# Scores of a head pair as products of 192 and 384 columns on two row halves, and an earlier copy of the attention product

## The chip, the cores and the metric

The kernel runs on one core of a Trainium2 chip. The metric is the device time of one execution in microseconds (us); the median of several executions counts.

## The reference

Top-k attention (8 batches, 8 heads, 576 rows, head size 64, k = 32), followed by a gated feed-forward part. Cut to what matters:

```python
scores = scale * np.matmul(q, k.transpose(0, 1, 3, 2))
kth = np.partition(scores, -32, axis=-1)[..., -32:-31]
scores = np.where(scores >= kth, scores, -1e9)
attn = exp(scores - max); attn /= attn.sum(-1)
x = (attn @ v), heads side by side                    # (8, 576, 512)
h = np.maximum(x @ w_in, 0)                           # 512 -> 1024
conv = conv_w[0]*h[s-1] + conv_w[1]*h[s] + conv_w[2]*h[s+1]
out = (h * sigmoid(conv)) @ w_out                     # 1024 -> 512
```

## The kernel before

Two heads form a pair, 32 pairs in all. A pair's 2 x 576 rows are cut into nine tiles of 128 rows: tiles 0, 2, 4, 6 hold 128 rows of the first head, tiles 1, 3, 5, 7 the same rows of the second, and tile 8 the last 64 rows of both heads, one head on each half of the partitions. That makes 288 tiles, and `iteration(it)` runs once for each: it writes out by hand, engine by engine, the work of several tiles that are at different stages. No scheduler moves anything, the written order is the engines' order. The feed-forward part of a finished batch is spread over the later iterations by a credit (`FEED`, `PE_CAP`); what is left over runs behind the last tile.

The names that matter here, in the order in which a tile meets them:

- `scores` (TensorE, L206, L211, L214): at an even tile it makes the scores of that tile and of the next, one head on rows 0 to 63 of the array, the other on rows 64 to 127, since a head has 64 elements. Both heads' first or last 512 columns are one product each (L211). The 64 columns that are left of each head are made together by one product over all 128 rows (L214), from an extra 128 columns of `k` that hold each head's edge beside zeros. An f32 product runs as two passes, each with its weight load. Tile 8 goes over quarters of the array (L206).
- `s_ps` is a PSUM tile of three banks of 512 columns. The first head's scores stand in columns 0 to 575, the second's in 960 to 1535, and in the middle bank between the two edges lie two corners of 128 columns, used in turn for the product of attention and values.
- `evacuate` (ScalarE, L220) copies a tile's 576 scores to `rows`; from there VectorE looks for the 32nd largest (L227, L247, L249, L275, L279), ScalarE makes `side` (L260) and the exponential (L272), GpSimd multiplies (L265), VectorE masks and sums (L285).
- `transposes` (TensorE, L298) puts the weighted tile into `pt`, `transposed` (ScalarE, L303, L305) copies it to `pT`, `tails` and `tailed` (L311, L315) do the same for the last columns.
- `av` (TensorE, L329, L332) multiplies `pT` with the values, two column halves at a time, into a corner of `s_ps`; `av_out` (ScalarE, L340) copies the corner to `xt` one iteration later.

In an iteration ScalarE runs `sides`, `evacuate`, `transposed`, `av_out`, then the exponential; TensorE runs `transposes`, feed-forward products (L396, L546), `tails`, `scores`, `av`. The scores of an even tile have to wait until ScalarE has read the middle bank, which means until the `xt` copy of the same iteration.

Of the kernel before, what the change touches and what calls it, by code (L numbers as in the profile page):

```python
# [21 lines left out]
P = 128  # L22
# [34 lines left out]
BANK = 512  # L57
# [8 lines left out]
def attend_and_feed(ctx: ExitStack, tc: tile.TileContext, q, k, v, weights, out, shared, finish=None):  # L66
    nc = tc.nc
    exact = finish is None
    v_main, v_tail = v
    B, NPAIR, _, S = q.shape  # L70
    D = P // 2
# [4 lines left out]
    SH = S // 2  # L76
    NI = S // P
    TAIL = S - NI * P
    MAIN = NI * P
    NBLK = 2 * NI + 1  # L80
    scale = 1.0 / float(D) ** 0.5
# [32 lines left out]
    s_ps = ps.tile([P, 3 * BANK], F32, name="s_ps", bufs=1)  # L114
# [3 lines left out]
    def bank(name):  # L118
        return ps.tile([P, BANK], F32, name=name, tag=name, bufs=1)

    def corner(i, w=P):
        return s_ps[:, BANK + TAIL + i * P:BANK + TAIL + i * P + w]

    scratch = []

# [72 lines left out]
    def scores(t):  # L198
        kx, qx = t.pc.nat["k"], t.pc.nat["q"]
        i = t.j // 2  # L200
        rows_of = [slice(h * D, (h + 1) * D) for h in range(2)]
        if t.j == 2 * NI:
            for to, n in ((0, MAIN), (MAIN, TAIL)):
                for h, d in enumerate(rows_of):
                    at = (to + TAIL * h) % S
                    nc.tensor.matmul(s_ps[rows_of[1 - h], to:to + n], lhsT=qx[d, 0:TAIL], rhs=kx[d, at:at + n],  # L206
                                     start=True, stop=True)
        elif t.j % 2 == 0:
            at = slice(TAIL + i * P, TAIL + (i + 1) * P)
            for h, d in enumerate(rows_of):  # L210
                nc.tensor.matmul(s_ps[:, 2 * h * BANK:(2 * h + 1) * BANK], lhsT=qx[d, at],  # L211
                                 rhs=kx[d, h * TAIL:h * TAIL + MAIN], start=True, stop=True)
            ends = s_ps[:, BANK:2 * BANK].rearrange("p (a c) -> p a c", c=TAIL)[:, 0:BANK // TAIL:BANK // TAIL - 1]
            nc.tensor.matmul(ends, lhsT=qx[:, at], rhs=kx[:, S:S + 2 * TAIL], start=True, stop=True)  # L214

    def evacuate(t):
        t.row = rows[:, t.n % XBUFS]
        x = t.x = t.row[:, 8:S + 8]
        at = 3 * BANK - S if t.j < 2 * NI and t.j % 2 else 0
        nc.scalar.copy(out=x, in_=s_ps[:, at:at + S])  # L220

    def chunk_ops(t):
# [77 lines left out]
    def transposed(t):  # L300
        st, j, tp = t.st, t.j, t.tp
        if j < 2 * NI:
            nc.scalar.copy(out=st.pT[:, j % 2], in_=tp.rearrange("p (i c) -> p i c", i=NI))  # L303
        else:
            nc.scalar.copy(out=st.pT[:, :, :, 0:TAIL].rearrange("p h i c -> p i h c"),  # L305
                           in_=tp.rearrange("p (i h c) -> p i h c", i=NI, h=2))
# [262 lines left out]
    parts, extra, outs_late, unready, ends = [], [], [], [], {}  # L569
# [57 lines left out]
    tiles = {}  # L627
# [83 lines left out]
    def iteration(it):  # L711
        nonlocal av_next, out_next, rec_next
        n = it + 3
        state.it = it
        pre, tA, tB, tC = (tiles.get(i) for i in (it + 2, it, it - 1, it - 2))
        tX, tD, tE = tiles.get(it - 3), tiles.get(it - 4), tiles.get(it - 5)
# [11 lines left out]
        if n < NT:  # L728
# [3 lines left out]
            t = Box()  # L732
# [5 lines left out]
            sides(tC)  # L738
        if pre is not None:
            evacuate(pre)  # L740
        if tE is not None:
            transposed(tE)
        outs, out_next = out_next, []
        for st in outs:
            av_out(st)
            if st.i == NI:
                norm_wait.append((it + NORM_LAG, st.pc))

        if exact:
            a_ops, b_ops = [], list(exact_ops(tB)) if tB is not None else []  # L750
# [67 lines left out]
        while pool_tasks and state.pool > 0.2 and pool_tasks[0][0] <= it:  # L818
# [3 lines left out]
            _, c, fn = pool_tasks.popleft()  # L822
# [11 lines left out]
        for it in range(-3, NT + 6):  # L834
            iteration(it)
    if finish is not None:
        finish(corner(2, 1)[0:1])
    while expands or contracts or any(x.waiting for x in lanes) or pool_tasks or tanh_next or tanh_now or gates:
        it += 1
        iteration(it)  # L840
# [67 lines left out]
def _layout(inputs):  # L908
    import numpy as np

    q, k, v = (np.asarray(inputs[name]) for name in "qkv")
    B, H, S, D = q.shape
    main = S // P * P

    def pairs(x, swapped):
        x = x.transpose(0, 1, 3, 2)
        heads = [np.concatenate([x[:, h, :, main:], x[:, h, :, :main]], axis=-1) if swapped(h) else x[:, h]
                 for h in range(H)]
        return np.stack(heads, axis=1).reshape(B, H // 2, 2 * D, S)

    ends = np.zeros((B, H // 2, 2, D, 2, S - main), k.dtype)
    for h in range(2):
        ends[:, :, h, :, h] = k[:, h::2, main:].transpose(0, 1, 3, 2)
    ends = ends.reshape(B, H // 2, 2 * D, -1)
    tails = np.zeros((B, H // 2, 2, S - main, 2, D), v.dtype)
    for h in range(2):
        tails[:, :, h, :, h] = v[:, h::2, main:]

    arrays = {
        "q": pairs(q, lambda h: True),  # L930
        "k": np.concatenate([pairs(k, lambda h: h % 2 == 1), ends], axis=-1),
        "v_main": v[:, :, :main].reshape(B, H // 2, 2, main // P, P, D).transpose(0, 1, 4, 2, 3, 5),
        "v_tail": tails.reshape(B, H // 2, 2 * (S - main), 2, D),
        "w_in": inputs["moe_w_in"],
        "conv_w": np.asarray(inputs["moe_conv_w"]).reshape(3, -1, P).transpose(2, 0, 1).reshape(P, -1),
        "w_out": inputs["moe_w_out"],
    }
    arrays = {name: np.ascontiguousarray(a) for name, a in arrays.items()}
    return {name: a.view(np.int64) if a.dtype == np.float64 else a for name, a in arrays.items()}
# [22 lines left out]
```

## Time and profile before

| | |
|---|---|
| three runs | 1128.35, 1132.26, 1133.33 us; median 1132.26 |
| profiled execution | 1132.29 us, of which 1130.4 us are the span in the trace |
| TensorE matmuls busy | 1022.8 us (90%) |
| VectorE busy | 1026.6 us (91%) |
| ScalarE busy | 994.4 us (88%) |
| GpSimd busy | 891.7 us (79%) |
| mean granted TensorE clock | 0.976 |

Busy time says how much of a stretch an engine was at work. A list of waits says who stood still and what ended it. The chain is the one path of work that ended last: time off the chain can vanish without moving the end. "issue" is time for which the profile shows no wait, and the ends of matmuls are modelled.

### The profile page before, as it was taken

To read this page: it belongs to the slowest core of one execution; us is meant where nothing else is said; L and a number is where in the kernel's file an instruction comes from. 1 tells how busy PE (TensorE), PEld (TensorE's weight loads), DVE (VectorE), ACT (ScalarE), POOL (GpSimd) and SP (SyncE) were. 2 spreads that over 40 slices of the span, in tenths; PEclk is the share of its full clock that TensorE was granted. 3 is DMA by queue.
4 is the path that set the end of the run, shared out by engine and by line. 5 is a ranking of instruction groups with operands and counts; after the bars stand their busy time and mean duration, and the time that the engine had idled before them with its cause. 6 is when DMAs were issued, how large, how long until landed. Compare 5 with 4: busy or idle time off the path is not lost.

```text
span 1130.4 us, 27192 instructions
## 1 busy us (share of the span) xinstructions
PE 1022.8 (90%) x7970; PEld 758.3 (67%) x7970; DVE 1026.6 (91%) x5768; ACT 994.4 (88%) x2342; POOL 891.7 (79%) x1078
## 2 busy tenths in 40 slices
PE   4656578889999999999999899999999999999997
PEld 1434345667677777777777677777677677777885
DVE  5998999999999999999999999999999999998651
ACT  5998888899999999999999999999999999998442
POOL 6999845879878897998887897978978897898300
PEclk9997888999999999999999999999999999999999
DMA  7321011111211101111111111111111110110001
GB/s 256 97 86 47 2 46 47 47 47 47 66 48 56 44 30 50 56 56 57 56 56 57 56 34 44 46 56 56 57 56 56 56 54 28 44 31 21 31 28 41
DMA packets 51694, 60.75 MB, mean 54 GB/s; under 512 B 9776, under 2 KB 30544, under 8 KB 51536
## 3 DMA queue, kind: packets, MB, share of 16 engines
q1 hardware_dynamic: 51536, 58.91, 16.4%
q8 instruction: 66, 1.08, 0.4%
q14 instruction: 92, 0.75, 0.2%
HBM read 49.31 MB, written 9.58 MB: 52 GB/s over the span
## 4 chain that ended last, share of the span: by engine, by line
PE 45%; DVE 36%; ACT 14%; POOL 2%; issue 2%; DMA 0%; SPq 0%; ACTq 0%; POOLq 0%
DVE cand L227 11%; PE mc L546 9%; DVE e L285 8%; PE me L396 8%; PE s_ps L329 6%; DVE z L275 6%; PE pt L298 5%; PE s_ps L211 5%; ACT weights_ps L272 3%; DVE cand L249 3%; PE s_ps L206 2%; PE s_ps L214 2%; ACT rows L220 2%; PE weights_ps L546 2%; DVE hot L279 2%; DVE rows L247 2%
## 5 line engine op out<-in xcount | busy, mean ns | idle before, releaser
L227 DVE MAX8 cand<-rows 128x8 f32<-128x82 f32 (+1 forms) x2016 | 453.0, 239 | 0.1
L265 POOL TENSOR_TENSOR z<-rows,side 128x579 f32<-128x579 f32 x288 | 347.5, 1207 | 127.5 <-ACT side L260 108.5
L285 DVE SCALAR_TENSOR_TENSOR e<-rows,kth,weights_ps 128x576 f32<-128x576 f32 x288 | 230.4, 800 | 0.2
L272 ACT ACTIVATE weights_ps<-rows,z 128x576 f32<-128x576 f32 x288 | 220.0, 764 | 8.2 <-DVE e L285 2.9
L260 ACT ACTIVATE side<-rows 128x576 bf16<-128x576 f32 x288 | 224.4, 779 | 0.3
L396 PE MATMUL me<-x_hi,wi 128*128 128x322 f32 (+1 forms) x928 | 218.6, 309 | 1.1 <-ACT g L410 1.1
L220 ACT COPY rows<-s_ps 128x576 f32<-128x576 f32 x288 | 183.5, 637 | 38.0 <-PE s_ps L332 21.0
L275 DVE MAX8 z<-z 128x8 f32<-128x576 f32 x288 | 214.2, 744 | 1.5 <-POOL z L265 1.5
L211 PE MATMUL s_ps<-k,q 64*128 64x512 f32 x512 | 151.4, 669 | 59.8 <-ACT xt L340 45.1
L298 PE MATMUL pt<-ident,e 128*128 128x128 f32 x1152 | 188.0, 287 | 2.1 <-DVE e L285 1.8
L546 PE MATMUL mc<-wo,split 128*128 128x512 f32 x684 | 187.1, 407 | 0.0
L329 PE MATMUL s_ps<-pT,vn 128*64 128x128 f32 (+1 forms) x2560 | 168.0, 276 | 12.7 <-ACT rows L220 12.6
L329 PEld LDWEIGHTS s_ps<-pT,vn 128*64 128x64 f32 x2560 | 131.9, 141 | 49.0 <-ACT rows L220 22.6
L396 PEld LDWEIGHTS me<-x_hi,wi 128*128 128x128 f32 x928 | 157.1, 189 | 2.3 <-ACT g L410 2.1
L303 ACT COPY pT<-pt 128x512 f32<-128x512 f32 x256 | 152.5, 596 | 4.2 <-PE pt L298 4.2
L298 PEld LDWEIGHTS pt<-ident,e 128*128 128x128 f32 x1152 | 131.9, 145 | 27.6 <-issue 14.7
L396 PE MATMUL me<-x_lo,wi 128*128 128x258 f32 (+1 forms) x464 | 138.4, 298 | 0.0
L546 PEld LDWEIGHTS mc<-wo,split 128*128 128x128 f32 x684 | 120.1, 189 | 20.0 <-issue 0.2
L429 POOL TENSOR_SCALAR t<-g,cr 128x256 f32<-128x256 f32 (+1 forms) x222 | 114.4, 515 | 0.0
L247 DVE MAX8 rows<-cand 128x8 f32<-128x21 f32 x576 | 109.4, 190 | 0.0
L214 PEld LDWEIGHTS s_ps<-k,q 128*128 128x128 f32 x256 | 39.9, 196 | 102.9 <-issue 102.9
L211 PEld LDWEIGHTS s_ps<-k,q 64*128 64x128 f32 x512 | 39.6, 189 | 90.6 <-ACT xt L340 58.6
(118 smaller groups left out, 1820.9 us busy)
## 6 DMA issues: line engine op xcount, KB each, us to landing
k<-in_k_dram SPq DMA_DIRECT2D x32, 352.0 KB
q<-in_q_dram SPq DMA_DIRECT2D x32, 288.0 KB
vn<-in_v_main_dram SPq DMA_DIRECT2D x32, 256.0 KB
rb<-row SPq DMA_DIRECT2D x64, 128.0 KB
out_dram<-o SPq DMA_DIRECT2D x24, 256.0 KB
raw<-in_w_in_dram SPq DMA_DIRECT2D x16, 256.0 KB
raw<-in_w_out_dram SPq DMA_DIRECT2D x16, 256.0 KB
vt<-in_v_tail_dram SPq DMA_DIRECT2D x32, 64.0 KB
```

What stands on the lines that cost most here:

```text
L211: nc.tensor.matmul(s_ps[:, 2 * h * BANK:(2 * h + 1) * BANK], lhsT=qx[d, at], rhs=kx[d, h * TAIL:h * TAIL + MAIN], start=True, stop=True)
L220: nc.scalar.copy(out=x, in_=s_ps[:, at:at + S])
L227: yield lambda c=c, at=at, n=n: nc.vector.max(out=t.cand[:, c:8 * CHUNKS:CHUNKS], in_=t.x[:, at:at + n])
L260: nc.scalar.activation(out=t.side[:, 2:S + 2], in_=t.x, func=AF.Sign, scale=-OVER, bias=t.row[:, 7:8], accum_out=t.cnt)
L265: nc.gpsimd.tensor_tensor(t.z[:, 8:S + 11], t.row[:, 6:S + 9], t.side, ALU.mult)
L272: nc.scalar.activation(out=e_ps, in_=t.x, func=AF.Exp, scale=scale, bias=t.shift)
L275: nc.vector.max(out=t.z[:, 0:8], in_=t.z[:, 10:S + 10])
L285: nc.vector.scalar_tensor_tensor(out=t.e, in0=t.x, scalar=kth[:, t.n:t.n + 1], in1=e_ps, op0=ALU.is_ge, op1=ALU.mult, accum_out=t.pc.sums[ ...
L298: nc.tensor.transpose(tp[:, i * P:(i + 1) * P], t.e[:, o + i * P:o + (i + 1) * P], ident)
L329: nc.tensor.matmul(a[r, 0:w], lhsT=st.pc.vn[:, h, i], rhs=st.pT[:, h if st.i < NI else 1 - h, i, 0:w], start=(i == 0), stop=False)
L396: nc.tensor.matmul(mm[:, 0:w], lhsT=wt, rhs=xx, start=(n == 0), stop=(n == len(ops) - 1))
L546: nc.tensor.matmul(mm[0:m], lhsT=x[:, i], rhs=wo[:, e, f], start=start, stop=stop)
```

## The change

Three things. The scores of an even tile become four products on the two row halves and no product over all rows: the first head's last 192 columns, the second's last 384, the first's first 384, the second's first 192. The layout of `s_ps` moves with it: corner 0 in columns 0 to 127, the first head's scores in 128 to 703, corner 1 in 704 to 831, the second head's in 832 to 1407. The first and the fourth product write the middle bank from different row halves, so a wait is put between them: the fourth waits on TensorE's own semaphore for the first. Tile 8 is cut at bank edges into 384, 128 and 64 columns in place of 512 and 64. And `k` loses its 128 extra columns (352 KB to 288 KB a load). Last, `av_out` stands ahead of `transposed` in the iteration.

```diff
-    def corner(i, w=P):
-        return s_ps[:, BANK + TAIL + i * P:BANK + TAIL + i * P + w]
+    def corner(i):
+        return s_ps[:, i * (P + S):i * (P + S) + P]
...
         if t.j == 2 * NI:
-            for to, n in ((0, MAIN), (MAIN, TAIL)):
+            for to, n in ((0, WIDE), (WIDE, MAIN - WIDE), (MAIN, TAIL)):
...
-            for h, d in enumerate(rows_of):
-                nc.tensor.matmul(s_ps[:, 2 * h * BANK:(2 * h + 1) * BANK], lhsT=qx[d, at],
-                                 rhs=kx[d, h * TAIL:h * TAIL + MAIN], start=True, stop=True)
-            ends = s_ps[:, BANK:2 * BANK].rearrange("p (a c) -> p a c", c=TAIL)[:, 0:BANK // TAIL:BANK // TAIL - 1]
-            nc.tensor.matmul(ends, lhsT=qx[:, at], rhs=kx[:, S:S + 2 * TAIL], start=True, stop=True)
+            made = []
+            for h, a, z in ((0, WIDE, S), (1, S - WIDE, S), (0, 0, WIDE), (1, 0, S - WIDE)):
+                to = (1 + h) * P + h * S
+                if len(made) == 3:
+                    tc.add_manual_dep(nc.tensor.nop().ins, made[0].ins.name,
+                                      mybir.DependencyInfo(mybir.DependencyClass.Sync, mybir.DependencyReason.DATA),
+                                      reason="two row tiles write one bank")
+                made.append(nc.tensor.matmul(s_ps[:, to + a:to + z], lhsT=qx[rows_of[h], at], rhs=kx[rows_of[h], a:z],
+                                             start=True, stop=True))
...
         if pre is not None:
             evacuate(pre)
-        if tE is not None:
-            transposed(tE)
         outs, out_next = out_next, []
         for st in outs:
             av_out(st)
             if st.i == NI:
                 norm_wait.append((it + NORM_LAG, st.pc))
+        if tE is not None:
+            transposed(tE)
```

TensorE, the scores of one even tile between the feed-forward products and the next transposes, before (`me<-ident` is `tails`, `pt<-ident` is `transposes`, `mc` the second feed-forward product):

```order
L546 MATMUL mc<-wo,split 128x512 [waits Pool_49]
L546 MATMUL mc<-wo,split 128x512 x6
L311 MATMUL me<-ident,e_4343 128x128 [waits Activation_49]
L211 MATMUL s_ps<-k,q 128x512 [waits Activation_49]
L211 MATMUL s_ps<-k,q 128x512
L214 MATMUL s_ps<-k,q 128x2x64
L298 MATMUL pt<-ident,e_4440 128x128 [waits DVE_49,PE_49]
```

The same place now:

```order
L551 MATMUL mc<-wo,split 128x512 [waits Pool_49]
L551 MATMUL mc<-wo,split 128x512 x6
L316 MATMUL me<-ident,e_4437 128x128 [waits Activation_49]
L218 MATMUL s_ps<-k,q 128x192 [waits Activation_49]
L218 MATMUL s_ps<-k,q 128x384 x2
L218 MATMUL s_ps<-k,q 128x192 [waits PE_49]
L303 MATMUL pt<-ident,e_4536 128x128 [waits DVE_49,Activation_49]
```

The edge product is gone, the fourth product waits for TensorE itself, and the next transposes now wait for the `pT` copy by a semaphore of their own, which the scores' wait covered before.

ScalarE, one iteration with an `xt` copy, before:

```order
L260 ACTIVATE side_109,cnt<-rows 128x576
L220 COPY rows<-s_ps 128x576 [waits PE_49]
L303 COPY pT<-pt 128x512 [waits PE_49]
L340 COPY xt<-s_ps 128x128
L272 ACTIVATE weights_ps<-rows,z 128x576 [waits DVE_49,Pool_49]
```

The same place now:

```order
L265 ACTIVATE side_109,cnt<-rows 128x576
L225 COPY rows<-s_ps 128x576 [waits PE_49]
L345 COPY xt<-s_ps 128x128
L308 COPY pT<-pt 128x512 [waits PE_49]
L277 ACTIVATE weights_ps<-rows,z 128x576 [waits DVE_49,Pool_49]
```

The `xt` copy has moved ahead of the `pT` copy and of the wait for the transposes that the `pT` copy carries. Neither list is otherwise changed there.

## Rows read from the trace of the kernel before

**Rows 1.** Windows: stretch, length, busy us (count) of PE, PEld, DVE, ACT, POOL, clock.
```profile
28.00:300.00 272.00, 207.15 (x1632) 142.50 (x1631) 256.74 (x1452) 243.56 (x586) 224.39 (x275) 0.91 0.16 50
300.00:1000.00 700.00, 682.91 (x5523) 509.95 (x5521) 677.15 (x3932) 665.27 (x1559) 599.67 (x708) 1.00 0.17 51
1030.00:1131.00 101.00, 91.62 (x557) 78.94 (x555) 48.84 (x113) 42.28 (x97) 23.81 (x28) 0.97 0.10 31
```

**Rows 2.** Waits of VectorE, 28 to 1030 us: total us, times, longest.
```profile
DVE hot L279 <- ACT weights_ps L457: 21.1, 32, 1.6
DVE hot L279 <- ACT weights_ps L272: 15.5, 17, 1.7
```

**Rows 3.** Waits of TensorE's matmuls, 28 to 1030 us.
```profile
PE s_ps L211 <- ACT xt L340: 45.1, 35, 3.4
PE s_ps L206 <- ACT xt L340: 10.7, 11, 1.9
```

**Rows 4.** Waits of ScalarE, 28 to 1030 us.
```profile
ACT rows L220 <- PE s_ps L332: 21.0, 33, 2.2
```

**Rows 5.** The page's chain by engine and by line.
```profile
PE 45%; DVE 36%; ACT 14%; POOL 2%; issue 2%; DMA 0%; SPq 0%; ACTq 0%; POOLq 0%
DVE cand L227 11%; PE mc L546 9%; DVE e L285 8%; PE me L396 8%; PE s_ps L329 6%; DVE z L275 6%; PE pt L298 5%; PE s_ps L211 5%; ACT weights_ps L272 3%; DVE cand L249 3%; PE s_ps L206 2%; PE s_ps L214 2%; ACT rows L220 2%; PE weights_ps L546 2%; DVE hot L279 2%; DVE rows L247 2%
```

**Rows 6.** The chain at its first change from the xt copy to scores: start, us.
```profile
42.41 0.18 ACT xt L340
42.59 0.04 issue
42.63 1.79 PE s_ps L211 x3
```

**Rows 7.** The chain at the second such change, ahead of a tile 8.
```profile
101.75 1.06 PE pt L298 x4
...
102.83 0.59 ACT pT L303
103.42 0.18 ACT xt L340
```

**Rows 8.** The chain at the last of these changes.
```profile
943.02 0.37 ACT pT L303
943.40 0.29 ACT xt L340
943.69 0.04 issue
943.73 1.13 PE s_ps L211 x4
```

**Rows 9.** Timeline of ScalarE at the same place: start, us, line, shapes.
```profile
942.40 0.62 ACT L220 COPY rows<-s_ps 128x576 f32<-128x576 f32 x1
942.92 0.59 ACT L303 COPY pT<-pt 128x512 f32<-128x512 f32 x1
```

**Rows 10.** Timeline of TensorE's matmuls over one even tile's scores, passes counted.
```profile
603.51 1.13 PE L211 MATMUL s_ps<-k,q 64*128 64x512 f32 x4
604.57 0.49 PE L214 MATMUL s_ps<-k,q 128*128 128x128 f32 x2
604.89 0.60 PE L298 MATMUL pt<-ident,e 128*128 128x128 f32 x4
```

**Rows 11.** Timeline of TensorE's matmuls, one attention product and its end.
```profile
940.61 1.09 PE L329 MATMUL s_ps<-pT,vn 128*64 128x128 f32 x16
941.53 0.39 PE L332 MATMUL s_ps<-pTt,vt 128*64 128x128 f32 x4
```

**Rows 12.** Timeline of TensorE's weight loads behind the scores of rows 10.
```profile
604.78 0.47 PEld L298 LDWEIGHTS pt<-ident,e 128*128 128x128 f32 x4
```

**Rows 13.** Timeline of TensorE's matmuls at the start of the kernel.
```profile
5.11 2.08 PE L211 MATMUL s_ps<-k,q 64*128 64x512 f32 x4 [5.11 <-DMA q<-in_q_dram]
7.12 0.80 PE L214 MATMUL s_ps<-k,q 128*128 128x128 f32 x2
```

More of the change, by code (lines that the diff above doesn't have):

```diff
@@ L78, in attend_and_feed @@
     TAIL = S - NI * P
+    WIDE = BANK - P
     MAIN = NI * P
@@ L202, in scores @@
         if t.j == 2 * NI:
-            for to, n in ((0, MAIN), (MAIN, TAIL)):
+            for to, n in ((0, WIDE), (WIDE, MAIN - WIDE), (MAIN, TAIL)):
                 for h, d in enumerate(rows_of):
                     at = (to + TAIL * h) % S
-                    nc.tensor.matmul(s_ps[rows_of[1 - h], to:to + n], lhsT=qx[d, 0:TAIL], rhs=kx[d, at:at + n],
+                    nc.tensor.matmul(s_ps[rows_of[1 - h], P + to:P + to + n], lhsT=qx[d, 0:TAIL], rhs=kx[d, at:at + n],
                                      start=True, stop=True)
@@ L218, in evacuate @@
         x = t.x = t.row[:, 8:S + 8]
-        at = 3 * BANK - S if t.j < 2 * NI and t.j % 2 else 0
+        at = P + (P + S if t.j < 2 * NI and t.j % 2 else 0)
         nc.scalar.copy(out=x, in_=s_ps[:, at:at + S])
@@ L836, in attend_and_feed @@
     if finish is not None:
-        finish(corner(2, 1)[0:1])
+        finish(corner(2)[0:1, 0:1])
     while expands or contracts or any(x.waiting for x in lanes) or pool_tasks or tanh_next or tanh_now or gates:
@@ L919, in pairs @@
         return np.stack(heads, axis=1).reshape(B, H // 2, 2 * D, S)
[L921 to L924, printed above, removed]
     tails = np.zeros((B, H // 2, 2, S - main, 2, D), v.dtype)
@@ L930, in _layout @@
         "q": pairs(q, lambda h: True),
-        "k": np.concatenate([pairs(k, lambda h: h % 2 == 1), ends], axis=-1),
+        "k": pairs(k, lambda h: h % 2 == 1),
         "v_main": v[:, :, :main].reshape(B, H // 2, 2, main // P, P, D).transpose(0, 1, 4, 2, 3, 5),
```

## The prediction

> **What bounds the kernel now.** I read the busy time by stretch first. From 300 to 1000 us, three fifths of the span, matmuls fill 683 of 700 us, VectorE 677 and ScalarE 665 [rows 1]. No engine alone is the bound: three engines at 95 to 98% hand work to each other, and what is lost is lost at the handovers. Behind 1030 us only feed-forward work is left, which the change doesn't touch. From 28 to 300 us TensorE is only 76% busy (207 of 272 us) at a mean granted clock of 0.91, between its two levels of 1.2 and 2.4 GHz, so there its work is short and slow at once.
>
> Then the waits. VectorE stands still for 36.6 us in 49 waits between 28 and 1030 us, all of them for ScalarE [rows 2]. That is the most that smoother handovers can give back as long as VectorE's own work stays as it is. TensorE's largest wait is for the `xt` copy: 45.1 us ahead of L211 and 10.7 us ahead of L206, together 55.8 us in 46 waits, 1.2 us each [rows 3]. ScalarE in turn waits 21.0 us for TensorE's attention product [rows 4].
>
> Last the chain, which tells what of this moves the end: TensorE has 45% of it, VectorE 36%, ScalarE 14% [rows 5]. Going through it from end to end I find 20 places where it passes from the `xt` copy straight to scores; the first is at 42 us [rows 6], the second at 103 us [rows 7], the last at 943 us [rows 8]. L211 has 5% of the chain, some 54 us; at 1.06 to 1.13 us each that is about 50 of the 128 score blocks [rows 5, 8, 10]. Those two counts carry the sum.
>
> **The earlier copy.** At 942.40 us ScalarE starts a `rows` copy, 0.52 us later the `pT` copy, 0.48 us later the `xt` copy, and at 943.73 us the scores start [rows 8, 9]. With the two exchanged, the `xt` copy starts where the `pT` copy did, 0.48 us earlier, and the scores with it. In the place at 103 us it is more: the chain runs through the transposes (1.06 us), the `pT` copy that waits for them (0.59 us) and the `xt` copy [rows 7]; the attention product ended ahead of the transposes, so the `xt` copy need not wait for them any more. I price all 20 at the smaller value: 20 x 0.48 = **9.6 us**. Nothing is added to ScalarE: the same copies run ahead of the same exponential. Queued behind the moved copy is the `pT` copy, now some 0.2 to 0.3 us later [rows 6, 8]; who waits for it are the next transposes, which stand behind a score block of over a microsecond and cover that, and the attention product of the next iteration. I cost it at nothing. The `rows` copy keeps its wait on TensorE, so I count nothing of the 21.0 us either [rows 4].
>
> **The score block.** Before, a block takes 603.51 to 604.89 us, 1.38 us from its first matmul to that of the next transposes: 1.06 us for the row halves with the change of array shape behind them, 0.32 us for the edge product [rows 10]. Both row halves run at once: in the attention product 16 passes of 128 columns, two at a time, take 0.92 us (940.61 to 941.53 [rows 11]), so a pass costs 0.115 us per 128 columns, 0.46 us for 512; four in a row would be 1.84 us, and L211 has them in 1.06. Now each half streams 576 columns in place of 512, in two passes; twice 64 more columns cost 0.115 us. The change of shape stays, only later: the transposes' first weight load, which stood beside the edge product and was 0.11 us ahead of its matmul (604.78 to 604.89 [rows 10, 12]), is now in the open, 0.11 us. Sum 1.06 + 0.115 + 0.11 = 1.285 us, 0.095 us less than 1.38, if the new wait costs nothing.
>
> The wait is the unknown. Behind it in TensorE's queue stand the fourth product and the next transposes, and ScalarE's `rows` copy waits for the fourth product. No row shows TensorE waiting for itself. From rows: the first product's two passes of 192 columns take 2 x 0.17 us behind a load of 0.11 us, its results arrive about 0.16 us later (L332 is modelled 0.39 us long, of which two pass lengths, 0.23 us, are its stream [rows 11]), and a semaphore takes 0.04 us to TensorE [rows 6]: 0.65 us into the block. The fourth product's load then takes 0.11 us, 0.76 us. Its row half is taken by the second product until 0.11 + 2 x 0.345 = 0.80 us. So it is just hidden, with 0.04 us to spare. From below the wait costs 0; above, if signalling and refilling the queue take 0.2 us longer, 0.16 us. I take 0.035 us and a block at 0.06 us less: 50 x 0.06 = **3.0 us**, with ends of +4.8 (0.095) and -3.3 us (a block 0.065 us longer).
>
> No row prices one more semaphore increment. The Trainium skill, "TensorE: Matmul & The Clock Gate", section "The cost: per-tile semaphore tail", puts about 26 ns on each; as an estimate that page alone would take 50 x 0.026 = 1.3 us from the gain, which no run here shows and which lies within the ends above.
>
> **The small edits.** Tile 8 gets a third pair of products but streams the same 576 columns; L206 has 2% of the chain, about 20 blocks [rows 5], and I take 0.5 us for the added starts (0 to 1). `k` is 64 KB smaller a load; 31 of 32 loads lie beside other work. The first doesn't: the first scores start at 5.11 us on the arrival of `q`, issued behind `k`, and their block then takes 2.8 us [rows 13]. The block's 0.095 us doubled for the slower clock, and as much again for the load: 0.4 us gained.
>
> **The sum.** 9.6 + 3.0 + 0.4 - 0.5 = 12.5 us. Each piece shortens one path, and others lie close behind: VectorE's mean wait is 0.75 us [rows 2], so a cut of 0.5 us mostly counts, but not each time. I keep nine tenths, 11 us. The profiled execution took 1132.29 us, its span 1130.4, and the median is 1132.26 us, so nothing is to be converted: **1121 us**.
>
> **Rivals.** *The path behind takes over.* ScalarE is 95% busy and must run the `pT` copy in any case ahead of the exponential that VectorE waits for; where its own work is late, scores that start sooner bring nothing. For it: all of VectorE's waits are for ScalarE. Against it: in 20 places the chain itself goes through TensorE. It would leave a third of the sum, 4 us: 1128 us.
>
> *The products run in written order.* If a product had to start both its passes before the next product starts, unequal lengths would hold the halves up: with passes of 0.17, 0.345, 0.345 and 0.17 us the second product starts at 0.17, the third at 0.52, and the last pass ends at 1.21 us of streaming in place of 6 x 0.17 = 1.03. The block is 1.285 + 0.18 = 1.46 us, 0.08 us longer than before: 50 x 0.08 = 4 us lost, 9.5 gained elsewhere (9.6 + 0.4 - 0.5): 1127 us. Against it: by the same rule the four passes of L211 would take three pass lengths of 0.46 us and a load, 1.5 us, and they take 1.06 [rows 10]. The Trainium skill, same page, section "The mechanism", says that matmuls start and end strictly in program order; by that this rival would hold, and the row above speaks against it for the two passes of a product.
>
> *Slower: the fourth product runs alone.* If the wait in effect lasts until all three products are done, the third ends 0.11 + 0.345 + 0.69 = 1.145 us into the block; then come 0.16 us of arrival, 0.04 us of semaphore, 0.11 us of load, 0.345 us of passes and 0.14 us to the transposes (0.03 for the shape, 0.11 for their load): 1.94 us, 0.56 us longer than before. On 50 blocks that is 28 us lost less 9.5 gained: 1151 us. The time is above that of before from 9.5 / 50 = 0.19 us a block on. For it: the wait stands in TensorE's only queue and holds all that follows. Against it: the wait is for the first product alone.
>
> *The clock.* With less to do TensorE may lose its clock: at 76% busy it had 0.91, at 98% 1.00 [rows 1]. A hundredth over 700 us is 7 us: 1128 us.
>
> **How the numbers follow.** The forecast, 6 to 18 us gained: 0.58. More than that, because the other 26 waits for the copy shorten too (46 x 0.48 = 22 us in all): 0.10. The path behind: 0.15. Written order: 0.06. The clock: 0.04. The fourth product alone: 0.07. Half a per cent, 5.7 us, is about what a measurement of this kernel can tell from no change. Faster by more: 0.58 + 0.10 and a little of the middle cases, 0.70. Within it: 0.20. Slower: 0.10, with 0.03 for what I don't see. The range reaches from 22 us less (46 waits and no loss) to the time of before: 1110 to 1133 us.
>
> **What would show it.** In the trace of after, the wait of the scores for the `xt` copy should fall from 55.8 to some 30 us or less, and VectorE's from 36.6 to some 25. The block, from its first matmul to the next transposes, should be 1.28 to 1.35 us; over 1.55 says that the fourth product doesn't overlap, which shows as a gap between its passes and the third's start. If the block is shorter and the waits fall, and the time stays, the path behind has it: ScalarE's copies will then stand on the chain where the scores stood. A granted clock under 0.99 from 300 us on would say the clock.

## The result, and the profile after

The changed kernel takes 1114.47 us (median of four runs, 1114.14 to 1115.11), the kernel before 1130.3 us in runs on the same chip. The ratio is 0.9862, 95% interval 0.9828 to 0.9895: 1.4% or some 16 us less, 12 to 19 by the interval. The forecast was 1121 us, 11 us less; the measured time lies inside the range. Of the 42 further runs of the kernel before that the experiments brought (1126.1 to 1133.2 us, median 1127.7), the nine at a mean granted clock of 0.973 or less took 1131.2 to 1133.2 us and the twenty at 0.98 or more 1126.1 to 1129.0; the changed kernel ran at 0.977 to 0.982. Two of the four runs of before that give the ratio took over 1132 us, so it sets the gain rather high: against the 42, and against those at a like clock, it is 12 to 14 us, close to the forecast. The profiled execution took 1114.6 us, its span 1112.7 us.

Busy time by stretch, in the columns of [rows 1]:

```profile
28.00:300.00 272.00, 208.04 (x1783) 160.61 (x1783) 263.45 (x1491) 249.11 (x602) 228.59 (x278) 0.93 0.17 53
300.00:1000.00 700.00, 685.19 (x5872) 553.67 (x5874) 685.15 (x3994) 670.84 (x1580) 611.01 (x724) 1.00 0.15 48
```

VectorE gets more done in the same stretches, 685.15 for 677.15 us in 700 and 263.45 for 256.74 in 272. The granted clock is 1.00 in both from 300 us on, and 0.93 for 0.91 ahead of that. So 14.7 us of its work that used to come behind 1000 us now comes before it.

The waits of VectorE, of TensorE and of ScalarE from 28 to 1012 us, against [rows 2 to 4]:

```profile
DVE hot L284 <- ACT weights_ps L462: 11.9, 21, 1.1
DVE hot L284 <- ACT weights_ps L277: 9.2, 12, 1.4
```

```profile
PE s_ps L218 <- ACT xt L345: 28.1, 28, 2.7
PE s_ps L334 <- ACT rows L225: 26.0, 20, 2.0
PE pt L354 <- ACT pT L310: 15.2, 10, 3.7
PE s_ps L207 <- ACT xt L345: 5.3, 7, 2.0
```

```profile
ACT rows L225 <- PE s_ps L337: 13.7, 27, 1.1
```

The scores' wait for the `xt` copy fell from 55.8 to 33.4 us. But TensorE waits more elsewhere: the attention product for the `rows` copy 26.0 us (12.6 before, line L329 there), and the transpose of the normalization for the `pT` copy 15.2 us (10.4 before). Most of both stands ahead of 300 us (21.9 of the 26.0 us and 13.4 of the 15.2). VectorE's wait fell from 36.6 to 21.1 us, ScalarE's for the attention product from 21.0 to 13.7.

The best single reading is one row of VectorE and one of ScalarE over the whole span. First VectorE's `hot` (`select`), which waits for what ScalarE writes into the PSUM tile `weights_ps`: the exponential (L272, after L277) and, in another part of the tile, a tanh of the feed-forward part (L457, after L462). The columns are busy time and mean, then the idle time ahead of it and who ended it. Before:

```profile
L279 DVE SCALAR_TENSOR_TENSOR hot<-weights_ps,cnt,z 128x10 f32<-128x10 f32 x288 | 62.4, 217 | 41.3 <-ACT weights_ps L457 21.1 <-ACT weights_ps L272 19.2
```

After:

```profile
L284 DVE SCALAR_TENSOR_TENSOR hot<-weights_ps,cnt,z 128x10 f32<-128x10 f32 x288 | 62.1, 216 | 26.0 <-ACT weights_ps L277 12.9 <-ACT weights_ps L462 11.9
```

The idle time fell by 15.3 us (41.3 to 26.0) and the span by 17.7. ScalarE's copies out of `s_ps`, before:

```profile
L220 ACT COPY rows<-s_ps 128x576 f32<-128x576 f32 x288 | 183.5, 637 | 38.0 <-PE s_ps L332 21.0 <-PE s_ps L214 12.9
L340 ACT COPY xt<-s_ps 128x128 f32<-128x128 f32 (+1 forms) x160 | 43.1, 269 | 0.0
```

After:

```profile
L225 ACT COPY rows<-s_ps 128x576 f32<-128x576 f32 x288 | 183.2, 636 | 21.0 <-PE s_ps L337 13.7 <-PE s_ps L218 6.0 <-ACT side L265 0.5
L345 ACT COPY xt<-s_ps 128x128 f32<-128x128 f32 (+1 forms) x160 | 41.9, 262 | 1.2 <-PE s_ps L337 1.2
```

ScalarE waits 22.2 us (21.0 + 1.2) for TensorE there in place of 38.0. So the gain reads like this: scores and attention products end sooner, ScalarE's copies wait less, what it writes into `weights_ps` comes sooner, VectorE waits less.

The chain passes from the `xt` copy to scores in 5 places in place of 20, the last of them here (start, us):

```profile
926.30 0.52 ACT rows L225
926.83 0.18 ACT xt L345
927.00 0.04 issue
927.05 1.30 PE s_ps L218 x6
```

The copy now stands behind the `rows` copy. And the score block of [rows 10], after:

```profile
602.63 1.30 PE L218 MATMUL s_ps<-k,q 64*128 64x192 f32 x8
603.86 0.66 PE L303 MATMUL pt<-ident,e 128*128 128x128 f32 x4
```

The block takes 1.23 us (602.63 to 603.86) for 1.38. The transposes behind it now start slowly, though, their load and their first pass together. Measured to the first transpose, the median of 90 blocks past 300 us is 1.229 us against 1.384 before, 0.155 us less; measured to the second, 1.394 against 1.493, 0.099 us less.

The scores also reach ScalarE sooner, by more than the block is shorter. Where its `rows` copy stands waiting for them, before:

```profile
660.10 1.13 PE L211 MATMUL s_ps<-k,q 64*128 64x512 f32 x4
661.73 0.64 ACT L220 COPY rows<-s_ps 128x576 f32<-128x576 f32 x1 [0.17 <-PE s_ps L214]
```

After:

```profile
665.23 1.30 PE L218 MATMUL s_ps<-k,q 64*128 64x192 f32 x8
666.57 0.64 ACT L225 COPY rows<-s_ps 128x576 f32<-128x576 f32 x1 [0.20 <-PE s_ps L218]
```

The copy starts 1.58 to 1.64 us into the block before, and 1.34 after: 0.25 to 0.30 us sooner. The prediction has no term for that.

### The profile page after: what moved, and what is told of

The parts are those of the page before. It is cut to its first block, busy times and chain, and to the rows that moved or that the text cites. A ratio compares the mean times of both kernels' runs of the same rounds, so it can differ in the third digit from the quotient of the medians.

```text
span 1112.7 us, 28088 instructions
## 1 busy us (share of the span) xinstructions
PE 1006.6 (90%) x8354; PEld 810.4 (73%) x8354; DVE 1024.9 (92%) x5768; ACT 989.6 (89%) x2342; POOL 892.1 (80%) x1078
## 4 chain that ended last, share of the span: by engine, by line
PE 45%; DVE 38%; ACT 12%; POOL 3%; issue 2%; DMA 0%; SPq 0%; ACTq 0%; POOLq 0%
DVE cand L232 12%; PE mc L551 10%; PE me L401 9%; DVE e L290 9%; DVE z L280 7%; PE pt L303 6%; PE s_ps L334 6%; PE s_ps L218 6%; DVE cand L254 3%; ACT weights_ps L277 3%; ACT side L265 2%; PE weights_ps L551 2%; DVE rows L252 2%; DVE hot L284 2%; ACT rows L225 2%; PE s_ps L207 2%
## 5 line engine op out<-in xcount | busy, mean ns | idle before, releaser
L277 ACT ACTIVATE weights_ps<-rows,z 128x576 f32<-128x576 f32 x288 | 219.6, 762 | 16.1 <-DVE e L290 7.5
L218 PE MATMUL s_ps<-k,q 64*128 64x384 f32 (+1 forms) x1024 | 172.5, 450 | 43.8 <-ACT xt L345 28.1
L225 ACT COPY rows<-s_ps 128x576 f32<-128x576 f32 x288 | 183.2, 636 | 21.0 <-PE s_ps L337 13.7
L303 PE MATMUL pt<-ident,e 128*128 128x128 f32 x1152 | 195.1, 293 | 2.6 <-DVE e L290 2.3
L218 PEld LDWEIGHTS s_ps<-k,q 64*128 64x128 f32 x1024 | 122.1, 191 | 86.2 <-ACT xt L345 37.0
L334 PEld LDWEIGHTS s_ps<-pT,vn 128*64 128x64 f32 x2560 | 130.7, 140 | 62.2 <-ACT rows L225 33.4
L303 PEld LDWEIGHTS pt<-ident,e 128*128 128x128 f32 x1152 | 125.1, 145 | 57.2 <-issue 28.9
L448 POOL TENSOR_TENSOR t<-t,t 128x256 f32<-128x256 f32 (+1 forms) x111 | 89.2, 803 | 9.2
```

The source lines that it names most:

```text
L218: made.append(nc.tensor.matmul(s_ps[:, to + a:to + z], lhsT=qx[rows_of[h], at], rhs=kx[rows_of[h], a:z], start=True, stop=True))
L277: nc.scalar.activation(out=e_ps, in_=t.x, func=AF.Exp, scale=scale, bias=t.shift)
L303: nc.tensor.transpose(tp[:, i * P:(i + 1) * P], t.e[:, o + i * P:o + (i + 1) * P], ident)
L334: nc.tensor.matmul(a[r, 0:w], lhsT=st.pc.vn[:, h, i], rhs=st.pT[:, h if st.i < NI else 1 - h, i, 0:w], start=(i == 0), stop=False)
```

## The experiments

All ratios are against the kernel before on the same chip. "Block" is the median from the first score matmul to the first of the next transposes, where nothing else is said.

**The two halves of the change.** The kernel before with the earlier copy alone:

```diff
-        if tE is not None:
-            transposed(tE)
         outs, out_next = out_next, []
         for st in outs:
             av_out(st)
...
+        if tE is not None:
+            transposed(tE)
```

> The kernel before with the xt copy ahead of the pT copy, and nothing else of the change: the score block, the layout and the wide k stay. Theory (two parts that add up, the copy the larger): the matmuls' wait for the copy falls from 55.8 to 30 to 36 us, the chain passes from the copy to scores in about 5 places instead of 20, the block stays 1.38 us, and the time falls by 9 us, to about 1121. Rival (the path behind takes over; what the change gained came from the block): the waits fall all the same, but the time stays within 4 us of before.

Measured: 1121.74 us, ratio 0.9936 (0.9916 to 0.9957), 7.2 us less by the ratio. TensorE's waits from 28 to 1050 us:

```profile
PE s_ps L211 <- ACT xt L340: 32.8, 31, 3.3
PE s_ps L329 <- ACT rows L220: 24.5, 20, 2.0
PE pt L349 <- ACT pT L305: 13.8, 9, 3.8
PE s_ps L206 <- ACT xt L340: 4.7, 5, 2.0
```

The `xt` wait falls by 18.3 us to 37.5, the attention product's wait for the `rows` copy grows by 11.9 and the normalization's by 3.4. Five sixths of the saved wait return in the two waits that follow. Yet 7 us are gained. ScalarE's wait fell (28.1 + 1.2 us for 38.0), nearly all of it in its wait for the attention product, L332; the one for the scores, L214, stayed (12.9 before):

```profile
L220 ACT COPY rows<-s_ps 128x576 f32<-128x576 f32 x288 | 183.2, 636 | 28.1 <-PE s_ps L332 13.1 <-PE s_ps L214 12.8
```

The changed kernel with the two copies in their old order, so the score edit alone:

```diff
+        if tE is not None:
+            transposed(tE)
         outs, out_next = out_next, []
...
-        if tE is not None:
-            transposed(tE)
```

> The changed kernel with the pT copy ahead of the xt copy again: new products, layout, wait and k alone. Theory: the block is 1.23 us as in the changed kernel, 0.155 us shorter to the first transpose and 0.10 us to the second; on some 50 blocks of the chain that is 5 to 8 us, so 1123 to 1126. Rival (the block does it all): 1115 to 1117. Rival (the copy does it all): 1130.

Measured: 1119.83 us, ratio 0.9924 (0.99 to 0.9947), 8.6 us less by the ratio. The time lies between those of the theory and of the first rival. The block is that of the changed kernel, 1.229 us. ScalarE's wait fell here in the other place, the wait for the scores:

```profile
L225 ACT COPY rows<-s_ps 128x576 f32<-128x576 f32 x288 | 183.5, 637 | 28.9 <-PE s_ps L337 20.4 <-PE s_ps L218 6.5 <-ACT side L265 0.5
```

The two parts together give 1.40%, the whole change 1.38%: they add up, within intervals of 0.21 and 0.24% either way on the parts.

**How many blocks count.** The order of the products changed so that the wait is for the third and the fourth runs alone:

```diff
-            for h, a, z in ((0, WIDE, S), (1, S - WIDE, S), (0, 0, WIDE), (1, 0, S - WIDE)):
+            for h, a, z in ((0, 0, WIDE), (1, S - WIDE, S), (0, WIDE, S), (1, 0, S - WIDE)):
...
-                    tc.add_manual_dep(nc.tensor.nop().ins, made[0].ins.name,
+                    tc.add_manual_dep(nc.tensor.nop().ins, made[2].ins.name,
```

> The changed kernel with the products in another order (the first head's first 384 columns, the second's last 384, the first's last 192, then the wait for that third product, the second's first 192), so that the wait is no longer covered. The fourth product then starts about 0.3 us after the third has streamed: the block grows by 0.68 us to 1.9 us. Theory (block time on TensorE counts on some 50 of 128 blocks): 34 us slower than the changed kernel, about 1148, at most 87 us. Rival (the copies and ScalarE's own work set the end, blocks are covered): under 1120.

Measured: 1163.29 us, ratio 1.0304 (1.0276 to 1.0331). One block:

```profile
614.12 1.88 PE L218 MATMUL s_ps<-k,q 64*128 64x384 f32 x8
615.94 0.66 PE L303 MATMUL pt<-ident,e 128*128 128x128 f32 x4
```

The median block is 1.813 us, 0.584 us longer than the changed kernel's; the time is 48.8 us longer, more than the 34 us of the theory. 48.8 / 0.584 = 84: it costs as much as if 84 of the 128 blocks counted in full.

The same with a smaller step, order kept, the wait for the second product:

```diff
-                    tc.add_manual_dep(nc.tensor.nop().ins, made[0].ins.name,
+                    tc.add_manual_dep(nc.tensor.nop().ins, made[1].ins.name,
```

> The changed kernel, order of the products kept, but the fourth product waits for the second instead of the first. The second's last pass stops 0.75 us into the block, its end is seen some 0.25 us later, and load and start take 0.13 us: the fourth starts at about 1.13 us in place of 0.76, and the block grows from 1.229 to about 1.5 us, 0.25 to 0.3 us more. Theory (the size of the block counts on about 84 of the 128 blocks, at small changes too): 21 to 25 us more than the changed kernel, 1135 to 1140 us, and VectorE's waits for ScalarE's weights grow by about as much. Rival (only the some 50 blocks of the chain count, and the 84 come from the large step of 0.584 us): 12 to 15 us more, 1126 to 1130 us.

Measured: 1139.18 us, ratio 1.0115 (1.01 to 1.0131). One block, and ScalarE's `rows` copies:

```profile
603.85 1.63 PE L218 MATMUL s_ps<-k,q 64*128 64x192 f32 x8
605.41 0.66 PE L303 MATMUL pt<-ident,e 128*128 128x128 f32 x4
```

```profile
L225 ACT COPY rows<-s_ps 128x576 f32<-128x576 f32 x288 | 183.1, 636 | 40.3 <-PE s_ps L218 19.9 <-PE s_ps L337 18.3
```

The block grows by 0.328 us to 1.557, the time by 24.7 us by the medians (28.6 by the ratios, give or take 4): as much as 75 to 87 blocks. The rival of 50 blocks falls, at this step too. The wait that grew most is the `rows` copy's for the scores, 19.9 us for 6.0.

These counts belong to the longer blocks. The chain of the changed kernel goes through the scores of 51 of the 128 blocks, that of the kernel before through 55; here it goes through 76, with the fourth product alone through 82. L218 has 11% of this kernel's chain, and 6% of the changed kernel's:

```profile
PE mc L551 13%; PE me L401 11%; PE s_ps L218 11%; PE pt L303 9%; PE s_ps L334 8%; DVE cand L232 8%; DVE e L290 6%; DVE z L280 5%; DVE cand L254 2%; ACT weights_ps L277 2%; PE weights_ps L551 2%; PE s_ps L207 2%; PE s_ps L337 2%; DVE hot L284 1%; DVE rows L252 1%
```

So a longer block draws more blocks onto the chain. What a shorter one is worth can't be read off these two kernels alone.

Set beside the kernel with the copy alone, which has the same order of copies, this kernel hands the scores over at nearly the same point of the block (1.66 us against 1.58 to 1.64), its second transpose comes 0.229 us later (1.722 against 1.493), and it takes 17.4 us more by the medians. That speaks for TensorE's time up to the transposes costing by itself, whatever the earlier hand-over of the scores is worth.

**Where the copy's saved wait returns.** The corner in use taken from behind the second head's scores, so that the attention product writes a bank that the first head's `rows` copy doesn't read:

```diff
-        a = st.a = corner(state.avs % 2)
+        a = st.a = corner(2)
```

> The changed kernel with the attention product always in columns 1408 to 1535 of s_ps, in the third bank, which the even tile's rows copy does not read. In the changed kernel TensorE's wait for that copy ahead of the attention product has grown from 12.6 to 26.0 us. Theory (what the earlier copy freed was in part given back in this wait, and it is on the path): the wait goes to about 0 and the time falls by 4 to 10 us, to 1105 to 1110. Rival (the wait only takes up slack that TensorE has ahead of VectorE): within 2 us of 1114.

Measured: 1114.68 us, ratio 0.9872 (0.985 to 0.9895), as the changed kernel. The attention product's wait is still there:

```profile
PE s_ps L334 <- ACT rows L225: 24.7, 20, 2.0
```

All 20 of these waits are for the first head's copy, which doesn't read that bank. The edit did not take the wait away, so neither its cause nor what it is worth is shown. A corner in a PSUM tile of its own was not tried.

The `xt` copy one place earlier still, ahead of the `rows` copy:

```diff
-        if pre is not None:
-            evacuate(pre)
         outs, out_next = out_next, []
...
+        if pre is not None:
+            evacuate(pre)
         if tE is not None:
             transposed(tE)
```

> The changed kernel with the xt copy moved once more, ahead of the rows copy. Theory (of the wait that the earlier copy saves, two thirds is given back because the next waits, the attention product's for the rows copy and the one for the pT copy, stand right behind): the wait of the scores for the xt copy falls from 33.4 to under 15 us, the attention product's for the rows copy grows from 26 to over 35 us, since that copy is now about 0.2 us later, and the time stays within 3 us of the changed kernel, 1112 to 1118 us. Rival (each place where the scores start sooner counts, as the prediction had it): another 0.2 to 0.5 us at some 20 places, 4 to 10 us less, 1105 to 1110 us.

Measured: 1113.9 us, ratio 0.9877 (0.9853 to 0.99), again as the changed kernel. TensorE's waits from 28 to 1012 us:

```profile
PE s_ps L218 <- ACT rows L225: 31.4, 31, 2.9
PE s_ps L334 <- ACT rows L225: 27.1, 20, 2.0
```

The scores' wait mostly changes its name (31.4 us for the `rows` copy, 28.1 for the `xt` copy in the changed kernel): the scores need both copies, and whichever comes last holds them. The attention product's wait did not grow as the theory had it.

The `xt` copy the other way, behind the exponential:

```diff
-        outs, out_next = out_next, []
-        for st in outs:
-            av_out(st)
...
         if tX is not None:
             expo(tX)
+        outs, out_next = out_next, []
+        for st in outs:
+            av_out(st)
```

> The changed kernel with the xt copy moved the other way, behind the exponential, one place later than it stood before the change. Theory (a copy moved by 0.5 us is worth some 7 us because other waits give back part of it): the exponential takes about 0.65 us and the wait for its inputs comes on top, so the scores start 0.65 us or more later than in the kernel with the score edit alone (1119.8 us); later starts are given back less and less, so nearly all of some 80 blocks that have a copy ahead of them (128 products of rows tiles, 160 blocks in all, most with a copy) pay: 80 x 0.65 = 52 us less the slack of those that did not wait, 1140 to 1180 us. Rival (path behind: ScalarE's order has little worth in either direction): within 10 us of the kernel with the score edit alone, 1115 to 1130 us.

Measured: 1177.18 us, ratio 1.0418 (1.038 to 1.0455): 57 us more than with the copy one place behind the `pT` copy (1119.83). VectorE's row:

```profile
L284 DVE SCALAR_TENSOR_TENSOR hot<-weights_ps,cnt,z 128x10 f32<-128x10 f32 x288 | 63.1, 219 | 83.6 <-ACT weights_ps L277 47.5 <-ACT weights_ps L462 34.4
```

That is in the theory's range. The position is worth a lot in one direction and little in the other: one place later costs 57 us, one place earlier gave 5 to 7 us, another one nothing. TensorE's granted clock is lower too, 0.82 from 28 to 300 us; how much of the 57 us hangs on that isn't separated.

The `rows` copy ahead of `side`:

```diff
-        if tC is not None and not exact:
-            sides(tC)
         if pre is not None:
             evacuate(pre)
+        if tC is not None and not exact:
+            sides(tC)
```

> The changed kernel with the rows copy ahead of side on ScalarE, so that the rows copy and the xt copy both come about 0.6 us sooner and side and all behind it later. Theory (what now holds the attention product is the rows copy, 26 us in 20 waits, and the scores the xt copy, 33 us): both waits fall by more than half. GpSimd's multiplication, which waits for side, starts some 0.6 us later, and if that is off the path the time falls to 1100 to 1110 us. Rival (GpSimd's result is what the exponential waits for, so side is on the path): the two waits of TensorE fall all the same, ScalarE's exponential waits for GpSimd instead, and the time rises to 1120 to 1150 us. I think the rival likelier.

Measured: 1133.54 us, ratio 1.0045 (1.0026 to 1.0063). ScalarE's `rows` copies:

```profile
L225 ACT COPY rows<-s_ps 128x576 f32<-128x576 f32 x288 | 185.6, 644 | 59.5 <-PE s_ps L337 41.5 <-PE s_ps L218 14.9
```

The time of the rival came, not its mechanism. The exponential waits no longer than elsewhere (9.0 us for all releasers together); the `rows` copy now comes before TensorE is done and waits 59.5 us for 21.0, time that `side` used to fill. Both expectations also had TensorE's two waits fall. The attention product's did, from 26.0 to 11.5 us; the scores' wait for the `xt` copy, which stands behind the waiting `rows` copy, grew from 33.4 to 53.3 us:

```profile
PE s_ps L218 <- ACT xt L345: 45.6, 39, 2.9
PE s_ps L207 <- ACT xt L345: 7.7, 9, 1.7
```

TensorE's part of the normalization behind the attention product:

```diff
-        for pc in recs:
-            norms(pc)
...
+        for pc in recs:
+            norms(pc)
```

> The changed kernel with TensorE's part of the normalization (one transpose at the end of a pair, which waits 15.2 us in 10 times for the pT copy) written behind the attention product of its iteration, where that copy is long done. Theory (the wait for the pT copy is one of the places to which the earlier xt copy gave its gain back, 4.8 of 15.2 us being new): the wait goes, and the time falls by 2 to 6 us, to 1108 to 1113 us. Rival (that wait is only the shape in which a later path shows itself; the next scores or the next transposes then wait instead): the time stays within 2 us of 1114.5 us, and another wait of TensorE grows by as much.

Measured: 1126.45 us, ratio 0.9981 (0.9966 to 0.9997): 12 us slower than the changed kernel, against both expectations. TensorE's and ScalarE's new waits:

```profile
PE pt L303 <- ACT rT L356: 12.9, 30, 1.4
```

```profile
ACT rT L356 <- PE pt L354: 15.2, 21, 1.0
```

The wait for the `pT` copy is gone, but ScalarE's copy of the norm now waits 15.2 us in its queue for the later transpose, and with it what stands behind it in that queue. VectorE's idle time ahead of `hot` is 37.8 us for 26.0.

**What TensorE's freed time is worth.** The changed kernel with more and with less feed-forward work in each iteration, and the kernel before with more:

```diff
-FEED = 1.42
+FEED = 1.47
```

> The changed kernel with a little more feed-forward work per iteration (1.47 for 1.42 units). Theory (what counts is VectorE's wait for ScalarE's weights, not TensorE's idle time: each product added between the transposes and the scores delays the scores): the wait grows by about what the shorter rest behind the last tile gives back; the time is within 5 us of the changed kernel, 1111 to 1120 us. Rival (the 0.155 us of TensorE that each block gave free is spare, 20 us in 128 blocks): 288 x 0.05 = 14 units of the rest move into the iterations at no cost, each unit about a product of 0.2 us or more by its share, 3 to 10 us less, 1105 to 1111 us.

> The changed kernel with a little less feed-forward work per iteration (1.37 for 1.42 units). Theory as in the run with 1.47: VectorE's waits fall, the rest behind the last tile grows by as much or more: 1112 to 1122 us. Rival (TensorE has time to spare now): the rest grows by the 3 to 10 us that the other run would gain, and nothing is won in the iterations, 1118 to 1125 us.

> The kernel before with 1.47 units of feed-forward work per iteration for 1.42. It tells whether a gain of the same step on the changed kernel comes from the time that the score edit freed: theory (the blocks are longer by 0.155 us and every delay of the scores counts): no gain or a loss, 1128 to 1140 us; rival (the amount is simply set too low for both): the same gain as on the changed kernel.

Measured: 1122.26 us (0.9965, 0.9951 to 0.9978) with 1.47; 1113.97 us (0.989, 0.9875 to 0.9905) with 1.37; the kernel before with 1.47: 1142.2 us (1.0132, 1.0117 to 1.0148). VectorE's row with 1.47 on the changed kernel, and then on the kernel before:

```profile
L284 DVE SCALAR_TENSOR_TENSOR hot<-weights_ps,cnt,z 128x10 f32<-128x10 f32 x288 | 62.2, 216 | 32.2 <-ACT weights_ps L462 18.3 <-ACT weights_ps L277 13.0
```

```profile
L279 DVE SCALAR_TENSOR_TENSOR hot<-weights_ps,cnt,z 128x10 f32<-128x10 f32 x288 | 62.7, 218 | 51.8 <-ACT weights_ps L457 25.3 <-ACT weights_ps L272 25.2
```

More work ahead of the scores costs 1.0% of the changed kernel (7.3 us by the profiled spans) and 1.3% of the kernel before (11.6 us by the spans, 15 by the ratio). The first lies above the ranges of both expectations, the second just above that of its theory. The freed time is not spare for more of this work. Less work gives nothing that can be told from the changed kernel. None of the experiments gave a version that is surely faster than the changed kernel.

**All kernels in one table**, from the profiled executions: the span, the idle time ahead of VectorE's `hot`, what is left of the span without it, and ScalarE's idle time ahead of its `rows` and `xt` copies.

| kernel | span | VectorE idle | rest | ScalarE idle |
|---|---|---|---|---|
| before | 1130.4 | 41.3 | 1089.1 | 38.0 |
| after | 1112.7 | 26.0 | 1086.7 | 22.2 |
| copy only | 1120.4 | 34.2 | 1086.2 | 29.3 |
| scores only | 1122.3 | 33.4 | 1088.9 | 28.9 |
| fourth product alone | 1162.5 | 68.7 | 1093.8 | 61.7 |
| wait for the second | 1137.5 | 47.5 | 1090.0 | 41.5 |
| corner in bank 2 | 1113.2 | 26.2 | 1087.0 | 21.7 |
| xt before rows | 1111.5 | 24.1 | 1087.4 | 20.7 |
| xt behind exponential | 1174.3 | 83.6 | 1090.7 | 74.3 |
| rows before side | 1132.5 | 42.2 | 1090.3 | 60.7 |
| norm behind products | 1124.6 | 37.8 | 1086.8 | 21.0 |
| feed 1.47 | 1120.0 | 32.2 | 1087.8 | 29.7 |
| feed 1.37 | 1112.5 | 27.5 | 1085.0 | 20.2 |
| before, feed 1.47 | 1142.0 | 51.8 | 1090.2 | 41.8 |

Each row is one execution; that of the scores only took 1124.1 us where the median of its runs is 1119.8. The rest lies between 1085.0 and 1093.8 us in all fourteen, while the span moves by 63 us. A part of this is arithmetic: VectorE is busy for 1022.5 to 1031.2 us in every kernel, so a longer span has to show as idle time of VectorE. What the table adds is where: nearly all of it stands ahead of one instruction. For steps of a few us the rest, which moves by up to 9 us itself, is too coarse. In twelve of the fourteen ScalarE's idle time is 2.5 to 10 us below VectorE's and moves with it. The two that break the pattern are those that move ScalarE's wait elsewhere: to the norm's copy (norm behind products), or from `side` to the `rows` copy (rows before side). That ScalarE's lateness is the cause in the others follows from the order of its queue and is not shown for each place.

## Why the prediction came out as it did

**The direction and the place: right.** The score block got shorter, the waits moved as described, and the time fell. VectorE's wait was said to be the most that there is to win "as long as VectorE's own work stays as it is", and 15.3 of the span's 17.7 us are this wait's fall. Its sentence "No engine alone is the bound" stands: VectorE's idle time moves, and ScalarE and TensorE decide how. Of the signs it named, the scores' wait for the `xt` copy fell to 33.4 us ("some 30 us or less"), VectorE's to 21.1 ("some 25"), and the block to 1.229 us, below the 1.28 to 1.35. That the sum came so near is in part luck: the copy was put at 9.6 us and gave 7.2, the block at 3.0 and gave 8.6, so the copy, put at three quarters of the sum, had less than half of it.

**"The earlier copy", 9.6 us: somewhat too large.** The run with the copy alone gave 7.2 us (4.9 to 9.5 by its interval). The 20 places were there and went to 5 (to 3 with the copy alone), but a path followed them: the sentence "The `rows` copy keeps its wait on TensorE, so I count nothing of the 21.0 us either" missed both what came back and what came on top. The attention product's wait for that copy doubled, and ScalarE's own wait for the attention product fell by 8 us with the copy alone (21.0 to 13.1). The `pT` copy, "I cost it at nothing", cost 4.8 us more of waiting ahead of the norm's transpose. Taking that wait away by moving the transpose was worse, so how much of the time it holds is not known.

**"The score block", 3.0 us: the term that was mis-sized.** The score edit alone gave 8.6 us (6.0 to 11.3), with the small edits' balance of -0.1 us in it. The size was too small: the new wait costs nothing, so the 0.035 us held back for it were not needed. The 0.095 us of the sum itself can be compared in two ways. To the first transpose the block is 0.155 us shorter. But that transpose now starts together with its load, and the second follows it by 0.165 us where transposes otherwise follow by 0.11; counted back by 0.11 from the second (1.394) the block ends at 1.284 us, and 1.285 was worked out. The count of some 50 was close for the chain it was read from, which goes through 55 blocks, but the two kernels with longer blocks cost as much as 75 to 87. Which correction carries the 8.6 us is not settled: 84 x 0.099 = 8.3, and 53 x 0.155 = 8.2 with the mean of the 55 and 51 blocks on the chains of before and after. The scores that reach ScalarE 0.25 to 0.30 us sooner, a term that the prediction left out, are in the 8.6 us too: the score edit alone cut ScalarE's wait for them from 12.9 to 6.5 us.

**The wait between the products: hidden, as worked out.** The prediction put the release 0.65 us into the block. In the block at 602.63 it came at 0.63 us, 0.205 us after the first product's second pass had stopped streaming (by its start and the 0.16 us that a pass of 192 columns takes), and the fourth product's load stands here, 0.71 us in (a load's row):

```profile
603.34 0.18 PEld L218 LDWEIGHTS s_ps<-k,q 64*128 64x128 f32 x1
```

Its first pass starts at 0.76 us, when the second product leaves that row half. With the wait for the second product the release came at 0.96 us, 0.209 us after that product's stream, and the whole difference stands in the block. There the fourth product's load and its first pass are 0.03 us apart; here they are 0.05, so the slack is some 0.02 us where 0.04 was worked out.

**The discount of a tenth** for paths close behind can't be judged: the two single parts give 1.40% and the whole 1.38%, and a tenth of the gain, some 0.14%, is less than their intervals.

**The rivals.** *The path behind* took part of the copy's gain (7.2 us of 9.6, and nothing for one place more) and left the time at 1114, not 1128. *Written order* falls: the block would have been 1.46 us and is 1.229. The second product's first pass starts 0.007 us into the block, ahead of the first product's second at 0.267. The Trainium skill, "TensorE: Matmul & The Clock Gate", section "The mechanism", has matmuls start and end strictly in program order. For passes of products on different row halves this trace does not agree, if a product's two passes follow each other in the program, which the trace doesn't tell. The Trainium skill, "TensorEngine Tiling (Array Packing)", section "Key Properties", says that tiles operate independently and may load weights and multiply in parallel; with that it agrees, by the load at 603.34 us beside the third product's passes. *The fourth product alone* was built as an experiment: with another order of the products, its block is 1.81 us where 1.94 was worked out, and it took 1163 us where 1151 was: the longer block costs as much as 84 and not 50. *The clock*, as a loss, falls: 1.00 from 300 us on, and 0.93 for 0.91 before that. Whether it has a part in the gain, as the spread of the runs of before suggests, isn't shown.

**The start.** The first scores start at 5.15 us (5.11 before), and the first `rows` copy at 7.48 us in place of 7.96: 0.48 us gained where 0.4 was forecast, in one execution of each.

## What to carry to other kernels

Before counting the places on the chain, look for the wait whose fall would be the gain: here the idle time ahead of VectorE's `hot`, and one row tells it for every variant. A busy engine's total idle time moves with the span in any case; the row is worth something because it names the place. A count of blocks on one chain holds for that kernel: with blocks longer by 0.33 and 0.58 us the chain itself went from 51 to 76 and 82 of 128 blocks. A kernel with a block made longer by a known amount measures what a longer block costs, and for a shorter one it is a guide only. Measure also when the result is ready for the next engine, and not only when the engine is free: here the two moved by 0.25 to 0.30 and by 0.10 to 0.155 us. And here a copy moved earlier in a full queue won only until the next copy that the same consumer needs: one place more gave nothing, and one place the other way cost 57 us.

## What the hardware showed that was not expected

- TensorE waiting for its own semaphore sees a product's end 0.205 and 0.209 us after the product's last pass stopped streaming, in two kernels; the fourth product's load followed 0.08 us later. The same wait was free on the first product and cost 0.328 us a block on the second.
- A copy one place later on ScalarE cost 57 us, while one place earlier gained 5 to 7. With it the granted clock from 28 to 300 us fell to 0.82, with TensorE 197.06 us busy of 272, against 0.93 at 208.04 us in the changed kernel.

```profile
28.00:300.00 272.00, 197.06 (x1547) 153.46 (x1548) 235.25 (x1329) 224.32 (x540) 203.17 (x251) 0.82 0.15 46
```

- Behind scores on row halves the first two transposes start 0.165 us apart (1.229 and 1.394 us into the block), where the next follow at 0.11 us and where, behind the edge product over all rows, these two did as well (1.384 and 1.493 us). That the change of the array's shape is the reason is likely, and no run isolates it.
